# Attention and channel mix on one core: loads of steps 1 to 6 on ScalarE's queue, normalising ahead of the reciprocals, two sums of weight quadrants moved

## The chip, the cores and the metric

The kernel runs on one core of a Trainium2 chip. The metric is the device time of one launch in microseconds; three runs of the kernel before took 910.71, 912.52 and 915.9 us, the median is 912.52 us.

## The reference

What is computed, cut to what matters (8 batches, 12 heads, 448 tokens, head size 64, model 768, hidden 1024, all float32):

```
scores = q @ k.T / 8
scores = cap * tanh(scores / cap)
attn   = softmax(scores)                       # per head
x      = (attn @ v), heads side by side        # (8, 448, 768)
xprev  = x shifted by one token
xk = mu_k * x + (1 - mu_k) * xprev
xr = mu_r * x + (1 - mu_r) * xprev
k  = relu(xk @ w_k)
out = sigmoid(xr @ w_r) * ((k * k) @ w_v)
```

## The kernel before

The 96 heads are taken as 48 pairs. `run` calls `step(i)` for i from 0 to 54; step i works on several pairs at once: the scores, tanh and exponentials of pair i, the product with the values of pair i-1, the reciprocals of its row sums, and the normalising and token mix of pair i-2. From the end of step 6 on each step also issues four pieces K of six matmuls each of the key product `xk @ w_k` for a batch whose six pairs are done. Behind the steps comes a second part, 112 slots long, that makes `(k*k) @ w_v` and `xr @ w_r` by seven products of quadrants in the place of eight.

Each engine works its instructions off in the order in which they are issued. That order is written out by hand as lists of words: `EVEN_0` and `ODD_0` for steps 0 to 5, `STEP_7` for step 6 (the name counts from one), `EVEN_6`/`ODD_6` and `EVEN`/`ODD` after them, `LAST` for steps 48 and 49. A digit behind a word is the group g of the 448 keys: groups 0 to 2 hold 128 keys each, group 3 holds the last 64 keys of two pairs and stands in even steps.

The words that matter here, with engine and line:

- `S` (TensorE, L249, L242): scores of a group into one of two PSUM tiles `s`. `tanh` (ScalarE, L255) frees that tile; `exp` (ScalarE, L267) follows in place.
- `V` (TensorE, L278, L288): product with the values, into one of two PSUM tiles `pv`. The tile of pair i-3 is taken over by pair i-1 in step i.
- `red` (VectorE, L297): sums of the exponentials of a group. `f` (VectorE, L488 to L497): one fifth of the unpacking of a 64-bit weight piece; four of the five issue work for the pieces 1 to 5, five for the wide ones from piece 6 on.
- `gather` (four transfers on SyncE's queue, L303): brings the sums of pair i-1 into one tile; `recip` (VectorE, L307 to L314): their reciprocals; `rec_store` (SyncE's queue, L317): writes them to HBM; `rec_load` (two transfers on SyncE's queue, L326): reads them back, spread over the partitions, into the one tile `r`.
- `norm` (VectorE, L330): multiplies pair i-2's `pv` by `r`; `mix_old` (ScalarE, L340): the old token's share, written back into `pv`; `mix_new` (VectorE, L345): the sum, after which `pv` is free; `x_high` (L97) and `x_low` (L107), both on GpSimd: the split of the mixed value into two parts for the matmuls.
- `load_v`, `load_qk`, `weight_load` (SyncE's queue, L182, L178, L452): the bulky loads, 256 KB, 448 KB and 384 or 768 KB. `weight_abs` (ScalarE, L464) reads the weight piece first, `weight_sum` (GpSimd, L504) ends its unpacking.
- `qk_high` (GpSimd, L97; as `qk_rise` on ScalarE, L101) and `qk_low` (GpSimd, L107): the same split for q and k of pair i+2.
- Around steps 48 and 49: `quad_sum` (VectorE, L731), the sums of quadrants of w_v, issued by the words `f` there, four for each half k of the rows; `w2_splits` (L737 on ScalarE, L738 on VectorE), a generator with 14 pairs of a cast and a subtraction, called from `run` and from the word `prep`; `relu` (ScalarE, L426), which frees a PSUM tile `kps` of the key product.

SyncE's queue waits in order too: a transfer that is not ready holds back all that are issued behind it. A transfer issued on ScalarE's queue stands in line among ScalarE's own instructions.

Of the kernel before, what the change touches and what calls it, by code (L numbers as in the profile page):

```python
# [17 lines left out]
B, H, S, D = 8, 12, 448, 64  # L18
NP = H // 2
# [5 lines left out]
NPAIR = B * NP  # L25
# [4 lines left out]
P = 128  # L30
U32 = mybir.dt.uint32
# [5 lines left out]
HC = DM // 2  # L37
# [26 lines left out]
ODD_0 = """load_v gather rec_load x_store weight_load S0 S1 V0 S2 V1 V2 V3 red3 f f f f f tanh0 exp0 red0  # L64
weight_sum tanh1 exp1 weight_abs red1 recip rec_store qk_high qk_low tanh2 exp2 norm red2 mix_old mix_new x_high x_low
load_qk weight_store"""
EVEN_0 = ODD_0.replace("V1", "V1 S3").replace(" red3", "").replace("red2", "red2 tanh3 exp3").replace("mix_new", "red3 mix_new")
# [4 lines left out]
STEP_7 = """load_v gather rec_load x_store weight_load weight_low S0 S1 V0 S2 V1 S3 V2 V3 f f f f f tanh0 exp0 red0  # L72
weight_sum tanh1 exp1 red1 recip rec_store tanh2 qk_rise exp2 norm red2 K K K K qk_low weight_abs tanh3 exp3 mix_old red3 mix_new x_high x_low
load_qk rec_load"""
LAST = """gather V recip rec_store norm rec_load K mix_old relu k_store prep mix_new x_high x_low gate_old
K f f f f f gate_new relu k_store prep K prep K relu k_store prep x_store tail_open"""
# [6 lines left out]
class Body:  # L83
# [93 lines left out]
    def load_part(self, i, c):  # L177
        self.nc.sync.dma_start(self.raw[i][:, c], self.qk[i // NP, i % NP][:, c])  # L178

    def load_v(self, i):  # L180
        t = self.rawv[i] = self.rawp.tile([P, 4, 2, D], F32, name="rv", bufs=3)
        self.nc.sync.dma_start(t.rearrange("p c h d -> p (c h d)"), self.v[i // NP, i % NP])  # L182
# [564 lines left out]
    def step(self, i, KS):  # L747

        nk = nq = 0
        if self.maxima and i < NPAIR and i % 2 == 0:  # L750
            for j in (i, i + 1):
                self.row_maxima(j)
        pair = dict(load_qk=i + 4, qk_high=i + 2, qk_low=i + 2, qk_rise=i + 2, load_v=i, S=i, tanh=i, exp=i, red=i)
        pair.update(dict.fromkeys("V gather recip rec_store".split(), i - 1))
        pair.update(dict.fromkeys("norm mix_old mix_new x_high x_low gate_old".split(), i - 2))
        pair.update(x_store=i - 3, gate_new=i - 3)
        for op in ((EVEN_0, ODD_0) if i < 6 else (STEP_7,) if i == 6 else (EVEN_6, ODD_6) if i < REST[0] else (LAST, LAST) if NPAIR <= i < NPAIR + 2 else (EVEN, ODD))[i % 2].split():
            j = pair.get(op)
            op, g = (op[:-1], (int(op[-1]),)) if op[-1].isdigit() else (op, ())
            if op in pair:  # L760
                j = pair[op] if j is None else j
                if op == "load_qk" and i == 0:
                    self.load_qk(3)
# [9 lines left out]
            elif op == "tail_open":  # L773
                self.tail_open(i)
            elif op == "f":
                if i in (QUADS + 3, QUADS + 5):
                    self.quad_sum(i - QUADS - 3)
                elif i <= NPAIR:
                    self.fill()
            elif op == "quad_load":  # L780
                if QUADS <= i < QUADS + 4:
                    self.quad_load(2 * (i - QUADS) + nq)
                    nq += 1
            elif op == "relu_early":
                if i % NP == 2:
                    self.relu()
            elif op == "weight_load":
                if i + 1 in KEYS or i + 1 in REST:
                    self.weight_load()
            elif op == "weight_abs":  # L790
                if i == 0:
                    self.guard()
                elif i in KEYS or i in REST:
                    self.weight_abs()
            elif op == "weight_store":
                if i == 0:
                    self.weight_abs()
                self.weight_store()
            else:
                getattr(self, op)()  # L800

    def run(self):
        tc, nc = self.tc, self.nc
        KS = NF * ND * 3 // NP // 4
# [5 lines left out]
        with ExitStack() as outer:  # L810
# [57 lines left out]
            for i in range(NPAIR + LAG):  # L868
                if i == tail:
# [110 lines left out]
```

## Time and profile before

| | before |
|---|---|
| three runs, us | 910.71, 912.52, 915.9 |
| profiled execution, us | 912.79 |
| its span, us | 910.9 |
| TensorE busy | 882.2 us, 97% |
| VectorE busy | 728.7 us, 80% |
| ScalarE busy | 627.1 us, 69% |
| GpSimd busy | 410.3 us, 45% |
| mean granted TensorE clock | 0.988 |

The span runs from the first to the last instruction; the execution's own time is 1.9 us longer. Shares over the whole span hide the stages: in the first 70 us TensorE has the gaps, and VectorE, ScalarE and GpSimd are all three busy for most of the time; from about 70 us on TensorE has few gaps. In the rows, "PE" is TensorE, "DVE" VectorE, "ACT" ScalarE, "POOL" GpSimd, "SPq" and "ACTq" the queues on which SyncE and ScalarE issue transfers.

### The profile page before, as it was taken

Reading aid. Unit: us, or ns where it says so; the run is one execution under the profiler, and the core shown is the slowest. Engines: PE = TensorE matmul, PEld = TensorE weight load, DVE = VectorE, ACT = ScalarE, POOL = GpSimd, SP = SyncE. Lnnn points to the kernel's source line nnn. Section 1 sums busy time; section 2 is a strip of 40 time slices with the busy share of each in tenths; the row PEclk is TensorE's granted clock in tenths of the full one; section 3 lists DMA queues with packets and bytes.
Section 4 is the critical chain, followed back from the end, with each engine's and each line's share of the span. In section 5 each row is a group of like instructions: output and inputs, shape, how many; then the busy total and the mean of one; then the engine's idle time right before and its main releaser. Section 6 shows DMA issues by size and latency. Waiting matters only on the chain.

```text
span 910.9 us, 15206 instructions
## 1 busy us (share of the span) xinstructions
PE 882.2 (97%) x5034; PEld 695.8 (76%) x5034; DVE 728.7 (80%) x1246; ACT 627.1 (69%) x899; POOL 410.3 (45%) x345
## 2 busy tenths in 40 slices
PE   7879999999999999999999999999999999999996
PEld 3236666666666666666666789999999999999996
DVE  6889986988998898898868656788878767777875
ACT  8898887877888878877877366566565535555553
POOL 4996674776776676676763200000000014443330
PEclk8899999999999999999999999999999999999999
DMA  5566646666667766766555355745454546766663
GB/s 179 175 198 186 196 158 190 195 213 195 198 197 207 216 181 196 216 199 189 184 186 182 125 202 157 237 158 176 146 163 153 181 139 192 217 218 216 222 217 112
DMA packets 123672, 170.04 MB, mean 187 GB/s; under 512 B 22592, under 2 KB 107712, under 8 KB 123584
## 3 DMA queue, kind: packets, MB, share of 16 engines
q1 hardware_dynamic: 114224, 154.10, 55.4%
q10 hardware_dynamic: 9360, 14.88, 4.5%
q8 instruction: 42, 0.69, 0.3%
q14 instruction: 46, 0.38, 0.1%
HBM read 109.91 MB, written 56.60 MB: 183 GB/s over the span
## 4 chain that ended last, share of the span: by engine, by line
PE 77%; DVE 8%; DMA 6%; ACT 5%; issue 2%; SPq 2%; POOL 1%; DVEq 0%; ACTq 0%; POOLq 0%
PE ps L622 39%; PE kps L419 19%; PE pv L278 9%; PE s L249 8%; DMA sq__194<-r 2%; DVE r L297 2%; ACT p L255 2%; PE pv L288 2%; DMA rec_d<-rs 1%; PE s L242 1%; DMA r<-rec_d 1%; ACT p L267 1%; SPq L303 1%; DVE xk L345 1%; DVE sq__194 L307 1%
## 5 line engine op out<-in xcount | busy, mean ns | idle before, releaser
L297 DVE TRANSPOSE_TENSOR_REDUCE r<-p 128x28 f32<-128x896 f32 (+1 forms) x192 | 183.1, 975 | 19.6 <-ACT p L267 19.3
L255 ACT ACTIVATE p<-s,scl_t 128x896 f32<-128x896 f32 x168 | 165.4, 997 | 39.4 <-PE s L249 29.8
L267 ACT ACTIVATE p<-p,cap_t 128x896 f32<-128x896 f32 x168 | 173.7, 1040 | 7.8 <-ACT ko L426 2.5
L419 PE MATMUL kps<-xkh,wkh 128*128 128x448 f32 x372 | 142.5, 383 | 4.0 <-ACT ko L426 3.7
L419 PE MATMUL kps<-xkh,wkl 128*128 128x448 f32 x372 | 136.7, 368 | 0.6 <-POOL wkl L107 0.6
L419 PE MATMUL kps<-xkl,wkh 128*128 128x448 f32 x372 | 136.6, 367 | 0.0
L586 POOL TENSOR_TENSOR s<-src 128x384 f32<-128x384 f32 x14 | 14.2, 1017 | 270.6 <-DVE lo L607 262.2
L278 PE MATMUL pv<-p,rv 128*64 128x448 f32 x576 | 125.3, 566 | 8.8 <-DVE xk L345 8.8
L622 PE MATMUL ps<-wvh,hi 128*128 128x384 f32 x392 | 131.2, 335 | 0.2 <-ACT xl L384 0.2
L622 PE MATMUL ps<-wvl,hi 128*128 128x384 f32 x392 | 131.1, 335 | 0.0
L606 ACT CAST hi<-s 128x512 fp32r<-128x512 f32 (+1 forms) x112 | 63.6, 567 | 89.9 <-PE ps L622 76.6
L607 DVE TENSOR_TENSOR lo<-s,hi 128x512 fp32r<-128x512 f32 (+1 forms) x112 | 71.1, 635 | 59.2 <-ACT hi L606 43.4
L107 POOL TENSOR_TENSOR qkl<-rqk,qkh 128x896 fp32r<-128x896 f32 x47 | 100.4, 2136 | 8.5 <-ACT qkh L101 5.0
L622 PE MATMUL ps<-wrh,hi 128*128 128x384 f32 x294 | 98.7, 336 | 0.3 <-DVE o L645 0.3
L622 PE MATMUL ps<-wrl,hi 128*128 128x384 f32 x294 | 98.6, 335 | 0.0
L419 PEld LDWEIGHTS kps<-xkh,wkh 128*128 128x128 f32 x372 | 70.2, 189 | 26.7 <-issue 13.8
L278 PEld LDWEIGHTS pv<-p,rv 128*64 128x64 f32 x576 | 37.0, 139 | 70.1 <-issue 53.3
L606 ACT CAST hi<-src 128x512 fp32r<-128x512 f32 (+1 forms) x84 | 47.7, 568 | 62.0 <-PE ps L622 59.1
L504 POOL TENSOR_TENSOR wsq<-wa,wsq 128x384 f32<-128x384 f32 (+1 forms) x40 | 54.2, 1354 | 75.9 <-DVE wsq L497 53.9
L622 PE MATMUL ps<-wvh,lo 128*128 128x384 f32 x392 | 83.8, 334 | 0.0
L419 PEld LDWEIGHTS kps<-xkl,wkh 128*128 128x128 f32 x372 | 70.2, 189 | 6.6 <-DVE xkl L107 0.4
L249 PEld LDWEIGHTS s<-qkh 64*128 64x128 f32 x288 | 27.8, 188 | 61.9 <-issue 23.6
(111 smaller groups left out, 1805.7 us busy)
## 6 DMA issues: line engine op xcount, KB each, us to landing
rqk<-qk SPq DMA_DIRECT2D x47, 448.0 KB
k_d<-ko ACTq DMA_DIRECT2D x64, 224.0 KB
src<-k_d SPq DMA_DIRECT2D x56, 256.0 KB
rv<-v SPq DMA_DIRECT2D x48, 256.0 KB
r<-rec_d SPq DMA_DIRECT2D x96, 112.0 KB
v_d<-o SPq DMA_DIRECT2D x56, 192.0 KB
src<-x_d SPq DMA_DIRECT2D x42, 256.0 KB
vl<-v_d SPq DMA_DIRECT2D x56, 192.0 KB
```

Of the source, the lines that this page charges most:

```text
L107: {"p": self.nc.gpsimd, "v": self.nc.vector}[e].tensor_sub(*a)
L249: nc.tensor.matmul(s[:, (h + i) % 2, 0:S], qk[a][p, k], qk[b][p, 0:S], start=(n == 0), stop=(n == 2))
L255: self.nc.scalar.activation(p32, self.S.pop((i, g))[:, :, 0:S], AF.Tanh, scale=self.scl_t)
L267: self.nc.scalar.activation(p32, p32, AF.Exp, scale=1.0 if self.maxima else self.cap_t)
L278: nc.tensor.matmul(pv[p, 0:S], v[:, g, h, :], ph[:, (h + i) % 2, :], start=(g == 0), stop=False)
L288: nc.tensor.matmul(self.PV[j][p, 0:S], v[t, 3, h, :], ph[t, j % 2, :], start=False, stop=True)
L297: self.nc.vector.tensor_reduce(out=r1[:, 0:RM].rearrange("p (x g) -> p x g", g=3)[:, :, g] if g < 3 else r1[:, RM:RC], in_=p32.rearrange(" ...
L419: nc.tensor.matmul(self.kps[fc][:, 0:S], w, m[:, dc, :], start=first, stop=last)
L504: {"p": self.nc.gpsimd, "v": self.nc.vector}[e].tensor_add(sq, f(a), sq)
L606: self.nc.scalar.copy(hi, x)
L607: self.nc.vector.tensor_sub(lo, x, f(hi))
L622: self.nc.tensor.matmul(o, a[:, c, :], w[:, c, :], start=first and k == 0, stop=last and k == len(todo) - 1, skip_group_check=True)
```

## The change

In steps 0 to 6 the lists are written anew. In steps 1 to 6 the three bulky loads go out on ScalarE's queue (`self.bulk`): the values and the q and k of a pair behind the first exponential, the weight piece behind the second. The q and k are loaded for pair i+3 in the place of i+4, and step 7 loads two pairs. `norm`, `mix_old` and `mix_new` stand ahead of `recip`, and `rec_load` right behind `rec_store`, so that `norm` uses what the step before has loaded. In steps 3 and 5 `x_high` becomes `x_rise`, on ScalarE. At the end of the attention, two of the four quadrant sums of the second half go from step 48 to step 49, behind `norm`, and the three weight splits ahead of step 49 go behind it, so that seven stand there in the place of four.

```diff
-ODD_0 = """load_v gather rec_load x_store weight_load S0 S1 V0 S2 V1 V2 V3 red3 f f f f f tanh0 exp0 red0
-weight_sum tanh1 exp1 weight_abs red1 recip rec_store qk_high qk_low tanh2 exp2 norm red2 mix_old mix_new x_high x_low
-load_qk weight_store"""
-EVEN_0 = ODD_0.replace("V1", "V1 S3").replace(" red3", "").replace("red2", "red2 tanh3 exp3").replace("mix_new", "red3 mix_new")
+ODD_0 = """gather x_store S0 S1 V0 S2 V1 V2 V3 red3 f f f f f tanh0 exp0 load_v load_qk red0
+weight_sum tanh1 exp1 weight_load norm weight_abs red1 mix_old mix_new recip rec_store rec_load qk_high qk_low x_rise x_low tanh2 exp2 red2
+weight_store"""
+EVEN_0 = ODD_0.replace("V1", "V1 S3").replace(" red3", "").replace("x_rise", "x_high").replace("red2", "red2 tanh3 exp3 red3")
...
-STEP_7 = """load_v gather rec_load x_store weight_load weight_low S0 S1 V0 S2 V1 S3 V2 V3 f f f f f tanh0 exp0 red0
-weight_sum tanh1 exp1 red1 recip rec_store tanh2 qk_rise exp2 norm red2 K K K K qk_low weight_abs tanh3 exp3 mix_old red3 mix_new x_high x_low
-load_qk rec_load"""
+STEP_7 = """gather x_store weight_low S0 S1 V0 S2 V1 S3 V2 V3 f f f f f tanh0 exp0 load_v load_qk red0
+weight_sum tanh1 exp1 weight_load norm red1 mix_old mix_new recip rec_store rec_load x_high x_low tanh2 qk_rise exp2 red2 K K K K qk_low weight_abs tanh3 exp3 red3"""
 LAST = """gather V recip rec_store norm rec_load K mix_old relu k_store prep mix_new x_high x_low gate_old
-K f f f f f gate_new relu k_store prep K prep K relu k_store prep x_store tail_open"""
+K f f gate_new relu k_store prep K prep K relu k_store prep x_store tail_open""", \
+    """norm K mix_old f f mix_new x_high x_low relu k_store prep K relu k_store prep K prep K relu k_store prep x_store"""
...
-        self.nc.sync.dma_start(self.raw[i][:, c], self.qk[i // NP, i % NP][:, c])
+        self.bulk.dma_start(self.raw[i][:, c], self.qk[i // NP, i % NP][:, c])
...
+    def x_rise(self, i):
+        self.x_high(i, "s")
...
+        self.bulk = self.nc.scalar if 0 < i < 7 else self.nc.sync
...
-        pair = dict(load_qk=i + 4, qk_high=i + 2, qk_low=i + 2, qk_rise=i + 2, load_v=i, S=i, tanh=i, exp=i, red=i)
+        pair = dict(load_qk=i + (3 if i < 7 else 4), qk_high=i + 2, qk_low=i + 2, qk_rise=i + 2, load_v=i, S=i, tanh=i, exp=i, red=i)
...
-                if op == "load_qk" and i == 0:
-                    self.load_qk(3)
+                if op == "load_qk" and i == 7:
+                    self.load_qk(10)
...
-                if i in (QUADS + 3, QUADS + 5):
-                    self.quad_sum(i - QUADS - 3)
+                if i in (QUADS + 3, QUADS + 5, QUADS + 6):
+                    self.quad_sum(i - QUADS - 3 & 2)
...
-                    self.w2 = self.w2_splits()
-                    for _ in range(3):
-                        next(self.w2)
                 self.prep_now = i in (tail + 1, tail + 2)
                 self.step(i, KS)
...
                 if i == tail:
-                    for _ in range(4):
+                    self.w2 = self.w2_splits()
+                    for _ in range(7):
                         next(self.w2)
```

`load_v` and `weight_load` take `self.bulk` in the same way; `tail` is step 49 and QUADS is 43. Three places show how the instructions now stand.

ScalarE in step 3, before (`p_490`, `p_497` and `p_514` are the groups 0, 1 and 2 of pair 3, L464 is `weight_abs`, L340 is `mix_old` of pair 1):

```order
L255 ACTIVATE p_490<-s,scl_t 128x896
L267 ACTIVATE p_490<-p_490,cap_t 128x896
L255 ACTIVATE p_497<-s,scl_t 128x896
L267 ACTIVATE p_497<-p_497,cap_t 128x896
L464 ACTIVATE wsq<-w_356 128x384
L255 ACTIVATE p_514<-s,scl_t 128x896
L267 ACTIVATE p_514<-p_514,cap_t 128x896
L340 ACTIVATE pv<-x_163,om_k 128x448
```

ScalarE in step 3, with the change (the groups are `p_484`, `p_495` and `p_523`; lines are three higher from L351 on):

```order
L255 ACTIVATE p_484<-s,scl_t 128x896
L267 ACTIVATE p_484<-p_484,cap_t 128x896
L182 DMA rv<-v 128x512
L178 DMA rqk<-qk 128x896
L255 ACTIVATE p_495<-s,scl_t 128x896
L267 ACTIVATE p_495<-p_495,cap_t 128x896
L455 DMA w_498<-wk 128x3x256
L467 ACTIVATE wsq<-w_407 128x384
L340 ACTIVATE pv<-x_163,om_k 128x448
L101 CAST xkh<-xk 128x448
L255 ACTIVATE p_523<-s,scl_t 128x896
L267 ACTIVATE p_523<-p_523,cap_t 128x896
```

Three loads have come in, and `mix_old` and the cast `x_rise` stand ahead of the last tanh, where `mix_old` stood behind the last exponential.

VectorE in step 3, before, from the sums of group 0 (L297) to `mix_new` (L345):

```order
L297 TENSOR_REDUCE r_1_198<-p_490 128x28
L297 TENSOR_REDUCE r_1_198<-p_497 128x28
L307 TENSOR_REDUCE sq__194<-sq__194 32x2x14
L309 TENSOR_REDUCE sr_196<-sq__194 32x28
L312 RECIPROCAL sr_196<-sr_196 32x28
L314 STREAM_TRANSPOSE rs<-sr_196 32x32
L330 TENSOR_TENSOR x_163<-pv,r 128x448
L297 TENSOR_REDUCE r_1_198<-p_514 128x28
L345 SCALAR_TENSOR_TENSOR xk<-x_163,mu_k,pv 128x448
```

VectorE in step 3, with the change, the same nine instructions:

```order
L297 TENSOR_REDUCE r_1_198<-p_484 128x28
L330 TENSOR_TENSOR x_163<-pv,r 128x448
L297 TENSOR_REDUCE r_1_198<-p_495 128x28
L345 SCALAR_TENSOR_TENSOR xk<-x_163,mu_k,pv 128x448
L307 TENSOR_REDUCE sq__194<-sq__194 32x2x14
L309 TENSOR_REDUCE sr_196<-sq__194 32x28
L312 RECIPROCAL sr_196<-sr_196 32x28
L314 STREAM_TRANSPOSE rs<-sr_196 32x32
L297 TENSOR_REDUCE r_1_198<-p_523 128x28
```

`norm` (L330) and `mix_new` (L345) have gone ahead of the four instructions of `recip`; the instructions ahead of these rows, two half sums and the four of `f`, stand where they stood.

VectorE from `norm` of pair 46 to `x_low` of pair 47, steps 48 and 49, before (L731 are the quadrant sums, L738 the subtractions of the splits, L357 `gate_new`):

```order
L330 TENSOR_TENSOR x_161<-pv,r 128x448
L345 SCALAR_TENSOR_TENSOR xk<-x_161,mu_k,pv 128x448
L731 TENSOR_TENSOR w_5088<-w_5089,w_5088 128x768
L731 TENSOR_TENSOR wa<-w_5090,w_5088 128x768
L731 TENSOR_TENSOR w_5089<-w_5090,w_5089 128x768
L731 TENSOR_TENSOR wsq<-wsq,wa 128x768
L357 SCALAR_TENSOR_TENSOR xg<-x_163,mu_r,xg 128x448
L738 TENSOR_TENSOR wvl_5694<-wa,wvh_5705 128x768 x2
L738 TENSOR_TENSOR wvl_5693<-w_5088,wvh_5704 128x768
L330 TENSOR_TENSOR x_163<-pv,r 128x448
L345 SCALAR_TENSOR_TENSOR xk<-x_163,mu_k,pv 128x448
L107 TENSOR_TENSOR xkl<-xk,xkh 128x448
```

The same stretch with the change:

```order
L330 TENSOR_TENSOR x_161<-pv,r 128x448
L345 SCALAR_TENSOR_TENSOR xk<-x_161,mu_k,pv 128x448
L734 TENSOR_TENSOR w_5088<-w_5089,w_5088 128x768
L734 TENSOR_TENSOR wa<-w_5090,w_5088 128x768
L360 SCALAR_TENSOR_TENSOR xg<-x_163,mu_r,xg 128x448
L330 TENSOR_TENSOR x_163<-pv,r 128x448
L734 TENSOR_TENSOR w_5089<-w_5090,w_5089 128x768
L734 TENSOR_TENSOR wsq<-wsq,wa 128x768
L345 SCALAR_TENSOR_TENSOR xk<-x_163,mu_k,pv 128x448
L107 TENSOR_TENSOR xkl<-xk,xkh 128x448
```

Two sums and three subtractions no longer stand ahead of `norm` of pair 47; two sums stand between it and its `mix_new`, and the subtractions follow `x_low`.

On SyncE's queue a step from 3 to 6 now reads: the four transfers of `gather`, `x_store`, `rec_store`, the two of `rec_load`.

## Rows read from the trace of the kernel before

**Rows 1.** Stretches: length, busy us of PE, PEld, DVE, ACT, POOL, granted clock, DMA.
```profile
21.40:68.10 46.70, 38.15 (x204) 14.47 (x202) 40.62 (x70) 41.62 (x48) 43.23 (x39) 0.89 0.57 180
...
50.60:56.30 5.70, 5.70 (x34) 2.41 (x34) 5.53 (x10) 5.46 (x7) 5.45 (x6) 1.00 0.36 124
...
530.00:533.80 3.80, 3.71 (x11) 3.32 (x12) 3.32 (x5) 3.12 (x7) 0.00 (x0) 0.55 1.01 337
```

**Rows 2.** Waits in 20 to 70 us: who for whom, total us, times, longest.
```profile
PE pv L278 <- DVE xk L345: 7.8, 4, 3.0
...
DVE sq__194 L307 <- DMA sq__194<-r: 3.8, 2, 2.1
```

**Rows 3.** Timeline of ACT, steps 2 to 7: start, length, instruction [idle before].
```profile
21.38 1.01 ACT L255 ACTIVATE p<-s,scl_t 128x896 f32<-128x896 f32 x1 [0.60 <-PE s L249]
...
40.79 1.01 ACT L255 ACTIVATE p<-s,scl_t 128x896 f32<-128x896 f32 x1 [0.78 <-PE s L249]
...
44.75 0.55 ACT L464 ACTIVATE wsq<-w 128x384 f32<-128x384 f32 x1
...
57.29 0.64 ACT L340 ACTIVATE pv<-x,om_k 128x448 f32<-128x448 f32 x1 [1.14 <-DVE x L330]
...
68.08 1.01 ACT L255 ACTIVATE p<-s,scl_t 128x896 f32<-128x896 f32 x1 [0.20 <-PE s L249]
```

**Rows 4.** Timeline of DVE, steps 1, 5 and 8.
```profile
21.00 0.20 DVE L314 STREAM_TRANSPOSE rs<-sr 32x32 f32<-32x32 f32 x1
...
51.03 0.53 DVE L491 TENSOR_SCALAR kps<-wsq 128x384 uint32<-128x384 uint32 x1
...
53.25 2.10 DVE L297 TRANSPOSE_TENSOR_REDUCE r<-p 128x28 f32<-128x896 f32 x2
55.27 0.48 DVE L307 TENSOR_REDUCE sq__194<-sq__194 32x28 f32<-32x336 f32 x1
...
56.66 0.60 DVE L330 TENSOR_TENSOR x<-pv,r 128x448 f32<-128x448 f32 x1
...
58.20 0.64 DVE L345 SCALAR_TENSOR_TENSOR xk<-x,mu_k,pv 128x448 f32<-128x448 f32 x1
...
89.44 0.68 DVE L345 SCALAR_TENSOR_TENSOR xk<-x,mu_k,pv 128x448 f32<-128x448 f32 x1 [1.67 <-ACT pv L340]
```

**Rows 5.** Timeline of ACT's queue: two transfers issued beside an exponential.
```profile
87.77 0.88 ACTq L432 DMA_DIRECT2D k_d<-ko  x2
```

**Rows 6.** Chain that ended last: landings of reciprocals on the way out and back.
```profile
25.78 4.04 DMA r<-rec_d
...
102.55 2.83 DMA rec_d<-rs
...
105.96 3.05 DMA r<-rec_d
...
113.33 1.28 DMA rec_d<-rs
```

**Rows 7.** Timeline of SyncE's queue: the two loads of pair 47's reciprocals.
```profile
512.50 1.12 SPq L326 DMA_DIRECT2D r<-rec_d  x2
```

**Rows 8.** Timeline of PE: products with values of steps 5 and 7, and step 51.
```profile
50.60 0.97 PE L278 MATMUL pv<-p,rv 128*64 128x448 f32 x4 [1.52 <-DVE xk L345]
...
69.32 2.48 PE L278 MATMUL pv<-p,rv 128*64 128x448 f32 x12 [0.66 <-DVE xk L345]
...
530.09 0.50 PE L419 MATMUL kps<-xkh,wkh 128*128 128x448 f32 x1 [2.14 <-ACT ko L426]
```

**Rows 9.** Timeline of DVE, step 48.
```profile
513.05 0.95 DVE L731 TENSOR_TENSOR w<-w,w 128x768 f32<-128x768 f32 x1
...
517.86 0.67 DVE L357 SCALAR_TENSOR_TENSOR xg<-x,mu_r,xg 128x448 f32<-128x448 f32 x1
```

**Rows 10.** Timeline of ACT, the splits behind step 49.
```profile
523.63 2.30 ACT L737 CAST wvh<-w 128x768 fp32r<-128x768 f32 x3
...
529.51 0.96 ACT L426 ACTIVATE ko<-kps 128x448 f32<-128x448 f32 x2
```

More of the change, by code (lines that the diff above doesn't have):

```diff
@@ L177, in load_part @@
     def load_part(self, i, c):
-        self.nc.sync.dma_start(self.raw[i][:, c], self.qk[i // NP, i % NP][:, c])
+        self.bulk.dma_start(self.raw[i][:, c], self.qk[i // NP, i % NP][:, c])
     def load_v(self, i):
         t = self.rawv[i] = self.rawp.tile([P, 4, 2, D], F32, name="rv", bufs=3)
-        self.nc.sync.dma_start(t.rearrange("p c h d -> p (c h d)"), self.v[i // NP, i % NP])
+        self.bulk.dma_start(t.rearrange("p c h d -> p (c h d)"), self.v[i // NP, i % NP])
     def qk_high(self, i, e="p"):
@@ L451, in weight_load @@
             src = self.wk.bitcast(U32)[d[0] * P:(d[-1] + 1) * P, 2 * c * P:2 * (c + 1) * P]
-            self.nc.sync.dma_start(w.rearrange("p (c n) t -> p c (n t)", n=P), src.rearrange("(c p) n -> p c n", p=P))
+            self.bulk.dma_start(w.rearrange("p (c n) t -> p c (n t)", n=P), src.rearrange("(c p) n -> p c n", p=P))
         else:
@@ L456, in weight_load @@
             src, c = (self.wr, c) if c < ND else (self.wv, c - ND)
-            self.nc.sync.dma_start(w.rearrange("p n t -> p (n t)"), src.bitcast(U32)[c * P:(c + 1) * P, 2 * h * HC:2 * (h + 1) * HC])
+            self.bulk.dma_start(w.rearrange("p n t -> p (n t)"), src.bitcast(U32)[c * P:(c + 1) * P, 2 * h * HC:2 * (h + 1) * HC])
         self.w_raw.append((n, w))
@@ L752, in step @@
                 self.row_maxima(j)
-        pair = dict(load_qk=i + 4, qk_high=i + 2, qk_low=i + 2, qk_rise=i + 2, load_v=i, S=i, tanh=i, exp=i, red=i)
+        pair = dict(load_qk=i + (3 if i < 7 else 4), qk_high=i + 2, qk_low=i + 2, qk_rise=i + 2, load_v=i, S=i, tanh=i, exp=i, red=i)
         pair.update(dict.fromkeys("V gather recip rec_store".split(), i - 1))
-        pair.update(dict.fromkeys("norm mix_old mix_new x_high x_low gate_old".split(), i - 2))
+        pair.update(dict.fromkeys("norm mix_old mix_new x_high x_rise x_low gate_old".split(), i - 2))
         pair.update(x_store=i - 3, gate_new=i - 3)
-        for op in ((EVEN_0, ODD_0) if i < 6 else (STEP_7,) if i == 6 else (EVEN_6, ODD_6) if i < REST[0] else (LAST, LAST) if NPAIR <= i < NPAIR + 2 else (EVEN, ODD))[i % 2].split():
+        for op in ((EVEN_0, ODD_0) if i < 6 else (STEP_7,) if i == 6 else (EVEN_6, ODD_6) if i < REST[0] else LAST if NPAIR <= i < NPAIR + 2 else (EVEN, ODD))[i % 2].split():
             j = pair.get(op)
@@ L803, in run @@
         tc, nc = self.tc, self.nc
+        self.bulk = nc.sync
         KS = NF * ND * 3 // NP // 4
```

## The prediction

> **What bounds the kernel now.** I read first the stretches, to find where TensorE is not full, then the waits there, then each engine's timeline step by step. In the stretch of steps 2 to 6, from 21.4 to 68.1 us, TensorE is busy for 38.2 of 46.7 us, while VectorE (40.6), ScalarE (41.6) and GpSimd (43.2) are each near full [rows 1]: three engines of nearly the same load, coupled step by step. TensorE's own wait there is for `mix_new`, which frees the tile of the products: 7.8 us in 4 waits [rows 2]. VectorE waits 3.8 us for gathered sums [rows 2]. From step 7 on TensorE is nearly full, so what these steps take longer or shorter is handed on to the end, as far as TensorE feels it.
>
> ScalarE's step starts are the reader's ruler: step 2 starts at 21.38, step 4 at 40.79, step 6 behind the instruction at 57.29, step 7 at 68.08 [rows 3]. A tanh and an exponential together take 1.98 us (two pairs from 40.79 to 44.75). ScalarE waits where `mix_old` waits for `norm`, 1.14 us in step 5 [rows 3].
>
> **The change, steps 1 to 6.** The durations on VectorE [rows 4]: the four of `f` 2.22 us (51.03 to 53.25), a sum `red` 1.01 (two until 55.27), `recip` 1.39 (until 56.66), `norm` 0.60, `mix_new` 0.64; a half-size sum I put at 0.55, an estimate from the 1.01. `mix_old` is 0.64 [rows 3].
>
> Before, `mix_old` was ScalarE's last work of a step, so nothing but its own queue stood between the groups. Now it stands ahead of the third tanh, and so do, on VectorE, the last sum of the step before, the four of `f`, the sum of group 0 and `norm`. That chain starts when the last exponential of the step before ends.
> - Even step: 1.01 + 2.22 + 1.01 + 0.60 = 4.84 us until `norm` is done. ScalarE would be there after two pairs and `weight_abs`, about 4.4, so it waits 0.4. Then `mix_old` 0.64 and two pairs 3.96: 9.44 us.
> - Odd step: two half sums, 2.22, 1.01, 0.60 make 4.93. Then the sum of group 1 and `mix_new`, 6.58; `x_rise` waits for that and takes about as long as `mix_old` on the same size, 7.2; one pair more: 9.2 us.
> - Step 2 waits for pair 0's reciprocals. They leave VectorE at 21.2 [rows 4], as before, since step 1 does nothing else there. The way out and back: landing 1.28 to 2.83 us from the issue of `rec_store`, 0.5 for the first `rec_load`, half of 1.12 [rows 7], and 3.05 to 4.04 from there [rows 6]: 4.9 to 7.4 us. I take 5.3, near the lower end, since no bulky load stands ahead on this queue any more. That is 5.1 into the step; with `norm`, `mix_old` and two pairs, 10.3 us.
> - Step 6: its ScalarE work is unchanged and had hardly a gap, 10.2 us (57.9 to 68.08). It now waits from 3.96, where two pairs are done, to 4.84: 11.1.
>
> Sum: 10.3 + 9.2 + 9.44 + 9.2 + 11.1 = 49.2 where 46.7 stood: step 7 starts 2.5 us **later** on ScalarE, at 70.6. Steps 3 to 5 pay for an early `norm` with waits on ScalarE.
>
> TensorE feels less of it. Its first products of step 7 started at 69.32, the last 0.66 of that a wait for `mix_new` [rows 8], and that wait goes. Now the second score group ahead of them waits for the tile that the last tanh of step 6 frees, 1 us ahead of step 7: 69.6. Six matmuls at 2.48 / 12 us each [rows 8] are 1.2 at most: 70.8, so **+1.5 us**. VectorE starts step 7 some 2 us late, but waits 1.67 us in step 8 for `mix_old` [rows 4], which takes up the rest. Bounds of this term: -0.7 (only the wait goes) to +2.5 (all of ScalarE's delay).
>
> What I cost at nothing:
> - The 18 loads in ScalarE's line. Two transfers took 0.88 us to issue [rows 5], beside an exponential; behind one they are covered. Uncovered, 3 x 0.44 a step less the 0.4 that ScalarE waits anyway would be 0.9 us a step, some 4.5 in all: the upper end. None has a buffer to wait for: each takes over a tile whose last reader was issued a step or more before.
> - `rec_load` holding SyncE's queue. It waits there for the landing of `rec_store`, and `gather` stands behind it. Counted from the end of a `recip`: 1.7 landing, 1.12 for `rec_load`, 2.2 for four issues at half of 1.12, and a landing of 2.2 between the 1.28 and 3.05 of [rows 6]: 7.2. The next `recip` starts 9.2 - 1.39 = 7.8 later. Cover 0.6; above that it is late.
> - `x_high` leaving GpSimd in steps 3 and 5: its splits of q and k were ready ahead of need.
>
> **The change, steps 48 and 49.** TensorE stood 2.14 us at 530.09 for a tile that `relu` frees [rows 8], and `relu` at 529.51 stood behind eight splits, 0.735 us each from 523.63 [rows 10]. After it the clock fell: 530 to 533.8 ran at 0.55 [rows 1]. Four sums took 4.81 us from 513.05 to 517.86 [rows 9]. With two there and `gate_new`, VectorE is free at 516.1; the loads of pair 47's reciprocals go out at 512.5 [rows 7], 0.5 + 3.05 later they are in: also 516.1. `norm` 516.7, `mix_old` beside two sums 519.1, `mix_new` 519.75, `x_high` 520.4. Then seven splits and four more from `prep`, eleven in all, 8.1 us: `relu` starts at 528.5 in place of 529.5. **-1.05 us**, and the gap shrinks to 1.1 us, or somewhat more where TensorE arrives sooner. A gap of 1.52 us [rows 8] was followed by a clock of 1.00, 50.6 to 56.3 [rows 1]; the one of 2.14 by 0.55. Mine is nearer to the first, so the clock holds: 0.45 x 3.8 = **-1.7 us**. Bounds: 0 (reciprocals 1 us later) to -2.75. The subtractions on VectorE end about when they did, so nothing behind is later.
>
> **Sum** against the profiled execution: 912.79 + 1.5 - 2.75 = **911.5 us**, 1.0 below the median of 912.52. The profiled execution lies 0.27 above that median. I take half a per cent, 4.6 us, as what a measurement of this kernel can tell from no change: below 908.0 faster, above 917.1 slower. Forecast: the same. With the bounds of both terms, 909.3 to 915.3.
>
> **Rivals.** *Slower: the reciprocals come late.* After a `recip` ends, 8.0 us into an odd step, the next `norm` wants them at 9.2 + 4.3: 5.5 us later; after an even step 5.9. At 5.3 they just fit. At the upper end, 7.4, each step waits 1.5 or 1.9, step 2 waits 2.1: 8.9 over five steps, 920.4 us; it passes half a per cent from about 6.6 us on. For it: both ends are measured in this kernel, and the bulky loads are still under way at the same time. Against it: 4.04 and 2.83 were taken with such loads ahead on the same queue. The Trainium skill, DMA: Bandwidth & Descriptors, section "Issuing engines are not separate DMA queues", has transfers from either queue run on the same 16 DMA engines and interleave, which would leave the landings where they were. No row of the kernel before shows the two queues loaded together; by that rule this rival holds. The same page's section on queues, rings and completion order lets each DMA engine take turns between queues, packet by packet, by which the small ones would pass: the forecast's 5.3.
>
> *Faster: ScalarE paces.* If the chain on VectorE is shorter than I sum it and no wait is left on ScalarE, its busy 41.6 us [rows 1] and two `x_rise` make 42.9: step 7 starts at 64.3, products some 0.2 later, 64.5 in place of 69.3, and 912.79 - 4.8 - 2.75 = 905.2 us. It takes about 60% of that to pass half a per cent. For it: ScalarE, TensorE and VectorE all had waits here, and the change aims at each. Against it: the order shows the four of `f` and two sums still ahead of `norm`, and their 4.8 us exceed ScalarE's 4.4.
>
> *Nothing happens in steps 1 to 6* because GpSimd, busy 43.2 of 46.7 [rows 1], holds the splits of q and k: then -2.75 alone, 910.0, still the same.
>
> **How the numbers follow.** Forecast 0.60, the third rival 0.08, slower 0.16, faster 0.16. The faster rival's lower part and the slower one's upper part are the 2 in 10 left out: 907 to 918. Faster by over 0.5%: 0.16; within: 0.68; slower: 0.16.
>
> **What would show it.** Right, step by step: ScalarE's `mix_old` waits for `norm` in every step from 2 to 6, and the third tanh follows it; step 7 starts near 70.6; TensorE's waits for `mix_new` in 20 to 70 us are gone; two transfers beside an exponential leave no gap; the gap ahead of the fifth key tile of the last batch is under 1.6 us and the clock in the 4 us behind it is 1.00. Wrong: a `norm` that waits for the landing of `r` in more than step 2 (the slower rival), step 7 before 67 us (the faster one), or a gap of 2 us with a lower clock behind it.

## The result, and the profile after

| | before | after |
|---|---|---|
| median, us | 911.73 (4 runs, 910.71 to 915.9) | 921.79 (4 runs, 920.66 to 924.04) |
| ratio | | 1.0105, 95% interval 1.0066 to 1.0144 |
| profiled execution, us | 912.79 | 920.8 |
| its span, us | 910.9 | 919.0 |
| mean granted clock | 0.988 | 0.985 |

The kernel before has one run more here than ahead of the prediction. The change makes the kernel slower by about 1%, 10 us; 911.5 was forecast, with 918 as the upper end. The profiled executions are 8.1 us of span apart.

Where these 8.1 us lie is read on TensorE, whose first twelve products with values in a step can be set side by side. The timeline of TensorE before, steps 7 (that one is in [rows 8]) and 8:

```profile
79.00 2.48 PE L278 MATMUL pv<-p,rv 128*64 128x448 f32 x12
```

The same products after, steps 7 and 8, and the one later stop, step 51:

```profile
74.70 4.13 PE L278 MATMUL pv<-p,rv 128*64 128x448 f32 x12
86.03 2.48 PE L278 MATMUL pv<-p,rv 128*64 128x448 f32 x12
...
538.25 0.47 PE L422 MATMUL kps<-xkh,wkh 128*128 128x448 f32 x1 [3.83 <-ACT ko L429]
```

At step 7 TensorE is 5.4 us late (74.70 to 69.32). The twelve products then take 4.13 us in place of 2.48, and from step 8 on it is 7.0 us late. It stays so to the last such products, of step 47 (512.32 to 505.21). The last 1.0 has come by the reciprocals of pair 47, which start at 517.77 in place of 509.68, ahead of all the work that the new tail moves. The stretches of steps 2 to 6, of these slow products and behind the late stop (columns as in [rows 1]):

```profile
20.90:74.80 53.90, 40.70 (x206) 15.26 (x204) 42.51 (x73) 43.02 (x50) 44.54 (x39) 0.87 0.51 163
74.80:79.00 4.20, 4.20 (x14) 1.21 (x16) 3.92 (x7) 3.99 (x5) 0.00 (x0) 0.59 0.40 120
538.20:542.00 3.80, 3.75 (x13) 3.40 (x14) 3.80 (x6) 3.34 (x6) 0.00 (x0) 0.68 0.56 194
```

Steps 2 to 6 take 53.9 us where 46.7 stood [rows 1] and 49.2 were forecast. The work in them is nearly the same; it is waits that grew, on every engine. The products of step 7 run at a granted clock of 0.59, which is mostly the lower of its two levels (1.2 of 2.4 GHz).

VectorE's timeline shows the wait, at the ends of the odd steps' reciprocals (L314) and the `norm` (L330) of the step behind:

```profile
21.58 0.20 DVE L314 STREAM_TRANSPOSE rs<-sr 32x32 f32<-32x32 f32 x1
28.25 0.62 DVE L330 TENSOR_TENSOR x<-pv,r 128x448 f32<-128x448 f32 x1 [2.23 <-DMA r<-rec_d]
...
41.24 0.20 DVE L314 STREAM_TRANSPOSE rs<-sr 32x32 f32<-32x32 f32 x1
...
47.46 0.63 DVE L330 TENSOR_TENSOR x<-pv,r 128x448 f32<-128x448 f32 x1 [0.42 <-DMA r<-rec_d]
...
60.79 0.20 DVE L314 STREAM_TRANSPOSE rs<-sr 32x32 f32<-32x32 f32 x1
68.15 0.63 DVE L330 TENSOR_TENSOR x<-pv,r 128x448 f32<-128x448 f32 x1 [1.80 <-DMA sq__194<-r]
```

From the end of a reciprocal to `norm` it is 6.5 (21.78 to 28.25), 6.0 and 7.2 us. 5.3 had been assumed. (The last wait is put down to a gather, but `norm` reads no sums: it waits for the counters of the two halves of `r`, whose loads went out from 64.09 on, and the second lands at 68.03.) The chain that ended last has the two legs of the first and the second of these; SyncE's queue shows the third's store and the loads that wait for it:

```profile
21.81 1.30 DMA rec_d<-rs
23.12 4.74 DMA r<-rec_d
...
41.47 1.25 DMA rec_d<-rs
43.33 3.93 DMA r<-rec_d
```

```profile
61.01 0.31 SPq L317 DMA_DIRECT2D rec_d<-rs  x1
64.09 1.12 SPq L326 DMA_DIRECT2D r<-rec_d  x2
```

The way out is short, as hoped, for the first two; for the third it is 3.1 us (61.01 to 64.09). On the way back a load of half of `r` takes 4.7 and 3.9 us, no less than with the bulky loads ahead on the same queue (4.04 and 3.05 in [rows 6]). From the first of the two loads to `norm` it is 5.1, 4.7 and 4.1 us, where 0.5 + 3.05 stood in the sum. Behind the late `norm` comes ScalarE, with a second stop of its own. Its timeline in step 2 and its step starts:

```profile
20.89 0.99 ACT L255 ACTIVATE p<-s,scl_t 128x896 f32<-128x896 f32 x1
...
27.94 0.39 ACTq L455 DMA_DIRECT2D w<-wk  x1
28.37 0.55 ACT L467 ACTIVATE wsq<-w 128x384 f32<-128x384 f32 x1 [3.42 <-DMA r<-rec_d]
...
33.43 0.99 ACT L255 ACTIVATE p<-s,scl_t 128x896 f32<-128x896 f32 x1
...
42.55 0.99 ACT L255 ACTIVATE p<-s,scl_t 128x896 f32<-128x896 f32 x1
...
52.74 0.99 ACT L255 ACTIVATE p<-s,scl_t 128x896 f32<-128x896 f32 x1
...
61.86 0.99 ACT L255 ACTIVATE p<-s,scl_t 128x896 f32<-128x896 f32 x1
...
74.81 0.99 ACT L255 ACTIVATE p<-s,scl_t 128x896 f32<-128x896 f32 x1
```

The steps take 12.54, 9.12, 10.19, 9.12 and 12.95 us. The odd ones are the forecast's 9.2; the even ones are 2.2, 0.75 and 1.85 longer than its 10.3, 9.44 and 11.1. And `weight_abs` (L467), which needs nothing of `r`, stands 3.42 us for its landing: the load of weights (L455) ahead of it in ScalarE's line went out only at 27.94. In the built program a transfer has one of eight completion counters (a semaphore that tells of its landing) in turn, whichever queue it is on, and is held until the transfer eight issues earlier has landed. For this load that is the first half of `r`, which lands at 27.86. The stop itself costs hardly anything here: `mix_old`, next in ScalarE's line, waits for `norm`, which ends at 28.87.

### The profile page after: what moved, and what is told of

It is laid out like the page before. It is cut to its first block, busy times and chain, and to the rows that moved or that the text cites. A ratio compares the mean times of both kernels' runs of the same rounds, so it can differ in the third digit from the quotient of the medians.

```text
span 919.0 us, 15199 instructions
## 1 busy us (share of the span) xinstructions
PE 885.4 (96%) x5034; PEld 696.4 (76%) x5034; DVE 726.3 (79%) x1246; ACT 627.7 (68%) x901; POOL 408.5 (44%) x343
## 4 chain that ended last, share of the span: by engine, by line
PE 80%; ACT 6%; DMA 6%; DVE 5%; issue 1%; SPq 1%; POOL 0%; ACTq 0%; DVEq 0%; POOLq 0%
PE ps L625 38%; PE kps L422 21%; PE pv L278 9%; PE s L249 8%; ACT p L255 2%; DMA sq__194<-r 2%; PE pv L288 2%; PE s L242 1%; DVE r L297 1%; DMA r<-rec_d 1%; ACT p L267 1%; DMA rec_d<-rs 1%; ACT wvh L740 1%; ACT ko L429 1%; DMA wvl<-w_d 1%
## 5 line engine op out<-in xcount | busy, mean ns | idle before, releaser
L297 DVE TRANSPOSE_TENSOR_REDUCE r<-p 128x28 f32<-128x896 f32 (+1 forms) x192 | 183.5, 975 | 21.4 <-ACT p L267 20.8
L610 DVE TENSOR_TENSOR lo<-s,hi 128x512 fp32r<-128x512 f32 (+1 forms) x112 | 70.6, 630 | 59.6 <-ACT hi L609 44.3
L609 ACT CAST hi<-src 128x512 fp32r<-128x512 f32 (+1 forms) x84 | 47.6, 567 | 61.2 <-PE ps L625 58.2
L249 PE MATMUL s<-qkh 64*128 64x448 f32 x288 | 65.7, 452 | 18.6 <-ACT p L255 10.4
```

The costliest lines, as they stand in the source:

```text
L249: nc.tensor.matmul(s[:, (h + i) % 2, 0:S], qk[a][p, k], qk[b][p, 0:S], start=(n == 0), stop=(n == 2))
L297: self.nc.vector.tensor_reduce(out=r1[:, 0:RM].rearrange("p (x g) -> p x g", g=3)[:, :, g] if g < 3 else r1[:, RM:RC], in_=p32.rearrange(" ...
L609: self.nc.scalar.copy(hi, x)
L610: self.nc.vector.tensor_sub(lo, x, f(hi))
```

## The experiments

Twelve kernels, in three sets, each beside the kernel before (medians 912.21, 912.01 and 912.21). "Step 7" and "step 8" say how many us after 69.32 and 79.00 the first products with values of these steps start in the profiled execution; where the second is larger by 0.9 or more, the products of step 7 ran at a low clock. The profiled execution is one of the runs, for `r` from v the fastest (916.45), for the old tail the slowest (922.51).

| run | median, us | ratio, 95% | step 7 | step 8 |
|---|---|---|---|---|
| the change | 921.79 | 1.0066 to 1.0144 | 5.4 | 7.0 |
| loads on SyncE | 921.66 | 1.0062 to 1.0135 | 7.1 | 8.8 |
| old tail | 919.21 | 1.0039 to 1.0086 | 6.9 | 8.6 |
| new tail alone | 912.71 | 0.9986 to 1.0022 | -0.9 | -0.9 |
| mixing at the end | 923.69 | 1.0069 to 1.0151 | 10.6 | 12.3 |
| `r` from v | 920.35 | 1.0077 to 1.0122 | 3.2 | 4.8 |
| reciprocals first | 934.54 | 1.0235 to 1.0282 | 21.4 | 22.3 |
| `norm` first alone | 917.56 | 1.0051 to 1.0088 | 5.4 | 5.4 |
| ScalarE's queue alone | 915.17 | 1.0023 to 1.0053 | 2.2 | 2.3 |
| `r` of pair 0 | 919.71 | 1.0060 to 1.0107 | 6.0 | 6.0 |
| the same, weights on SyncE | 919.12 | 1.0050 to 1.0085 | 4.8 | 6.3 |
| weights on SyncE | 919.35 | 1.0054 to 1.0094 | 4.8 | 4.8 |
| `r` of pair 0, all on SyncE | 916.12 | 1.0028 to 1.0059 | 1.4 | 1.4 |

Theory 1 was at first: the way of the reciprocals, out and back, ends last. Theory 2: the loads in ScalarE's line.

**Loads back on SyncE's queue.**

```
-        self.bulk = self.nc.scalar if 0 < i < 7 else self.nc.sync
+        self.bulk = self.nc.sync
```

> The change with the bulky loads of steps 1 to 6 back on SyncE's queue, at the places where the new lists issue them; order of norm, mix and reciprocals as changed. Theory 1 (the reciprocals come too late for an early norm, and the third tanh stands behind norm): nothing of the loss goes, 918 to 922 us, steps 2 to 6 on ScalarE still take 52 to 55 us where the kernel before takes 46.7. Theory 2 (the loads in ScalarE's line hold ScalarE: its weight load waits for the landing of the reciprocals and all behind it stands): the three waits of 3.4, 1.0 and 2.9 us ahead of weight_abs go, 912 to 915 us.

921.66 us, as with the change: to move the loads back gives nothing, against theory 2. The chain that ended last, the store that step 6 waits for:

```profile
60.81 5.55 DMA rec_d<-rs
```

and VectorE's `norm` behind it:

```profile
69.85 0.63 DVE L330 TENSOR_TENSOR x<-pv,r 128x448 f32<-128x448 f32 x1 [3.44 <-DMA sq__194<-r]
```

Now the small store takes 5.55 us, behind three bulky loads issued on its queue from 58.2 to 59.6 us; the way back is 3.5 (66.38 to 69.85). In all 9.1 us from the end of the reciprocals, 7.2 with the change. In steps 2 and 4 it is 6.2 and 6.3 us, 6.5 and 6.0 with the change: there time moves from one leg to the other.

| us, `norm` of step | 2 | 4 | 6 |
|---|---|---|---|
| the change: from the store to the loads of `r`, from there to `norm` | 1.3, 5.1 | 1.3, 4.7 | 3.1, 4.1 |
| loads on SyncE: the same | 1.9, 4.2 | 2.8, 3.5 | 5.6, 3.5 |

**The tail as before; the new tail alone.** In the first, `LAST`, the branch of `quad_sum` and the calls of `w2_splits` are before's in the changed kernel; in the second the reverse.

```
-                if i in (QUADS + 3, QUADS + 5, QUADS + 6):
-                    self.quad_sum(i - QUADS - 3 & 2)
+                if i in (QUADS + 3, QUADS + 5):
+                    self.quad_sum(i - QUADS - 3)
...
```

> The change in steps 0 to 6, but quadrant sums, splits and list of steps 48 and 49 as before. By the trace of the change its products with values run 7.1 us behind the kernel before up to step 48 and its key product of the last batch 8.15 us behind afterwards, so the new end costs about 1 us: 920 to 921 us, gap ahead of the fifth key tile back near 2.1 us. By the forecast's term the new end gains 1.0 to 2.7 us: 922.5 to 924.5 us. If the 1 us is chance of one execution: no difference, 921 to 922 us.

> The kernel before with only the end of steps 48 and 49 changed. By the forecast's term 909 to 911 us; by the reading of the change's trace (the reciprocals of pair 47 land some 5 us after their load is issued, norm of pair 47 waits for them, relu stands behind eleven splits) about 1 us slower than before, 912 to 913.5 us, with a gap of 3 to 4 us ahead of the fifth key tile.

With the old tail 919.21 us, below all three figures named, its interval overlapping the change's; the new tail alone is no different from before, 1.0004. So the loss is in steps 0 to 6, and the tail's forecast gain isn't there. Why, by the second's timelines of VectorE, ScalarE and TensorE:

```profile
517.23 0.63 DVE L331 TENSOR_TENSOR x<-pv,r 128x448 f32<-128x448 f32 x1 [1.37 <-DMA r<-rec_d]
...
528.76 0.96 ACT L427 ACTIVATE ko<-kps 128x448 f32<-128x448 f32 x2
...
529.35 0.47 PE L420 MATMUL kps<-xkh,wkh 128*128 128x448 f32 x1 [2.91 <-ACT ko L427]
```

This execution is 0.86 us ahead at the reciprocals of pair 47 (508.82 against 509.68). The loads of `r` go out at 511.64, and `norm` waits for them to 517.23: 5.6 us, 0.5 + 3.05 assumed. `relu` at 528.76 is then 0.75 ahead of 529.51, 0.1 later than the lead alone gives. TensorE, which ends its work ahead of the stop 1.5 us sooner than before, stands 2.91 us, and the clock is low behind it as before.

**Mixing back at the end of the step**, loads on ScalarE's queue, `norm` first:

```
-weight_sum tanh1 exp1 weight_load norm weight_abs red1 mix_old mix_new recip rec_store rec_load qk_high qk_low x_rise x_low tanh2 exp2 red2
+weight_sum tanh1 exp1 weight_load norm weight_abs red1 recip rec_store rec_load qk_high qk_low tanh2 exp2 red2 mix_old mix_new x_rise x_low
```

> The change with mix_old and mix_new of steps 1 to 6 back behind the last exponential (x_rise, x_high behind them), norm still ahead of recip, loads still on ScalarE's queue. Theory 1: ScalarE's third tanh no longer stands behind norm, steps 2 to 6 take 46 to 48.5 us, 912 to 915 us. Theory 2: the weight load is still in ScalarE's line ahead of the third tanh and still waits for the landing of the reciprocals, so ScalarE still stands some 3 us in steps 2 and 6: 917 to 921 us.

923.69 us: theory 1's forecast for it fell, and theory 2's 921 is passed. ScalarE's timeline, step 3:

```profile
38.11 0.33 ACTq L178 DMA_DIRECT2D rqk<-qk  x1
38.50 1.01 ACT L255 ACTIVATE p<-s,scl_t 128x896 f32<-128x896 f32 x1 [4.97 <-DMA r<-rec_d]
```

A tanh stands 4.97 us behind a load of q and k that itself waits for `r`. With the early mixing that stop is hidden, since `mix_old` waits for the same `r`; without it, it shows. So both theories have a part, and theories A (the way of `r`) and D (both, one behind the other) were put to the next two sets.

**`r` that waits for nothing.** In the first, `r` of pairs 0 to 5 is read from the input v; its output has other magnitudes, and its six times spread from 916.45 to 922.61, so its trace is used.

```
+    def r_early(self, i):
+        r = self.up.tile([P, S], F32, name="r", bufs=1)
+        for h in range(2):
+            self.nc.sync.dma_start(r[HALF[h]], self.v[i // NP, i % NP][h:h + 1, 0:S].to_broadcast([64, S]))
+        self.R[i] = r
...
-weight_sum tanh1 exp1 weight_load norm weight_abs red1 mix_old mix_new recip rec_store rec_load qk_high qk_low x_rise x_low tanh2 exp2 red2
+weight_sum tanh1 exp1 weight_load norm weight_abs red1 mix_old mix_new r_early recip rec_store rec_load qk_high qk_low x_rise x_low tanh2 exp2 red2
```

> The change, but in steps 1 to 6 the tile r of pairs 0 to 5 is loaded from rows of the input v, behind mix_new and ahead of recip, in place of the stored reciprocals (so these six pairs are normalised by other numbers; the reciprocals are still computed and stored). Same size and number of loads, but nothing to wait for. Theory A: the loop recip, rec_store, rec_load, norm, mix_new, recip paces steps 2 to 6, since norm now stands ahead of recip and its r is out and back in 6.0 to 7.2 us; a turn is 9.6 us. Then no norm waits for r in steps 2 to 6, the steps take the 49.2 us of the prediction or less, the first twelve products with values of step 7 start near 70 to 71 us (74.7 with the change), and the time is 912 to 916 us. Theory B: the early mixing chain on VectorE and ScalarE is what is long, and the waits for r only lie beside it: products at 73 us or later, 919 to 922 us.

No `norm` waits for `r` in steps 2 to 6, yet step 7 is still 3.2 us late: by this trace A's part is 2.2 of 5.4. ScalarE stood 0.55 to 1.75 us ahead of the weights in each step (a load of weights, and what it waited for). The second reads the stored reciprocals of pair 0 for pairs 1 to 5 (`self.rec_d[0]` in `r_early`), and pair 0 its own; two more move loads in it.

> The change, but in steps 2 to 6 the tile r of pairs 1 to 5 is loaded from the stored reciprocals of pair 0, behind mix_new and ahead of recip (these five pairs are normalised by pair 0's sums; their own reciprocals are still computed and stored). As the run with r from v, with numbers of the usual size. Theory D (two causes, one behind the other: norm's wait for r, and behind it ScalarE standing at the load of weights that it issues itself, 0.5 to 1.7 us a step ahead of weight_abs): the first products of step 8 start 4 to 5.5 us after the 79.0 us of before (86.0 with the change), 916 to 919 us. Theory A (r alone): within 1.5 us of 79.0, 911 to 914 us.

> As r of pair 0, and the loads of weights of steps 1 to 6 go out on SyncE's queue at the same place of the program (values, q and k stay on ScalarE's). Theory D: ScalarE's gaps ahead of weight_abs fall under 0.3 us each, products of step 8 within 2 us of 79.0, 911 to 914.5 us: below the run with r of pair 0 by 2 us or more. Theory A: no different from the run with r of pair 0.

> As r of pair 0, and all bulky loads of steps 1 to 6 on SyncE's queue at their places of the change. Theory D: as with the weights alone on SyncE's queue, 911 to 914.5 us, if the queue as such costs nothing. Theory E: on one queue the gathered sums and r stand behind the bulky loads, so recip waits for gather by 1 us or more in several steps: 915 to 920 us.

With `r` of pair 0 and the loads on ScalarE's queue: 919.71 us, 6.0 late at both steps: A's 911 to 914 us is out, D's ends, 919 us and 5.5 late, are passed by a little, since pair 0 waits 3.09 us for its own `r`. ScalarE in step 4, the load of weights held:

```profile
49.06 0.41 ACTq L463 DMA_DIRECT2D w<-wk  x1
49.57 0.54 ACT L475 ACTIVATE wsq<-w 128x384 f32<-128x384 f32 x1 [1.99 <-POOL wkl L107]
```

With the weights' loads on SyncE's queue these stops are gone, as D said, but not the time, against it: pair 0 waits for its own `r`, 4.40 us in step 2, and starts 7.3 us behind the first load of it (22.74 to 30.06), and the clock is low at step 7 (3.89 us for the twelve products). With all loads on SyncE's queue the same `norm` waits 1.2 us. That kernel's step starts and two of its `mix_old` on ScalarE, steps 2 to 7, and its products on TensorE, steps 7 and 8:

```profile
21.51 1.01 ACT L255 ACTIVATE p<-s,scl_t 128x896 f32<-128x896 f32 x1 [0.64 <-PE s L249]
...
32.00 0.99 ACT L255 ACTIVATE p<-s,scl_t 128x896 f32<-128x896 f32 x1
...
37.09 0.64 ACT L348 ACTIVATE pv<-x,om_k 128x448 f32<-128x448 f32 x1 [0.60 <-DVE x L338]
...
41.13 0.98 ACT L255 ACTIVATE p<-s,scl_t 128x896 f32<-128x896 f32 x1
...
50.68 0.99 ACT L255 ACTIVATE p<-s,scl_t 128x896 f32<-128x896 f32 x1
...
59.81 0.99 ACT L255 ACTIVATE p<-s,scl_t 128x896 f32<-128x896 f32 x1
...
64.85 0.64 ACT L348 ACTIVATE pv<-x,om_k 128x448 f32<-128x448 f32 x1 [1.00 <-DVE x L338]
...
70.86 0.98 ACT L255 ACTIVATE p<-s,scl_t 128x896 f32<-128x896 f32 x1
```

```profile
70.73 2.48 PE L278 MATMUL pv<-p,rv 128*64 128x448 f32 x12
80.40 2.48 PE L278 MATMUL pv<-p,rv 128*64 128x448 f32 x12
```

Here the prediction's chain stands as it was summed: steps of 10.49, 9.13, 9.55, 9.13 and 11.05 us (49.35; forecast 49.2) and products at 70.73 (70.8). Beside the run with all loads on SyncE's queue and each pair's own `r`, it is the plainest pair of the series: to open the loop of `r` takes off 5.5 us (921.66 to 916.12), and step 7 is 1.4 us late in place of 7.1. The median, 916.12, is above D's 914.5, and within E's 915 to 920, but not by E's waits: no `recip` of steps 2 to 6 waits for `gather`. 1.4 us are lost by step 8 and some 2.4 more in the tail of the profiled execution, where TensorE stands 3.88 us.

**Weights alone on SyncE's queue**, `r` as in the change (`self.nc.sync` in place of `self.bulk` in the two loads of `w`):

> The change with one edit: the loads of weights of steps 1 to 6 go out on SyncE's queue at the same place of the program. Theory D: norm still waits for its own r, and mix_old behind it, so that taking only the second cause away gives back under 2.5 us: 918.5 to 922 us. If ScalarE's own loads were the main cause: 912 to 916 us.

919.35 us, as D has it: with its stop taken away, `norm` still waits for `r` (2.67, 0.38 and 1.21 us).

**The order alone.** The reciprocals ahead of `norm` in the changed kernel:

```
-weight_sum tanh1 exp1 weight_load norm weight_abs red1 mix_old mix_new recip rec_store rec_load qk_high qk_low x_rise x_low tanh2 exp2 red2
+weight_sum tanh1 exp1 weight_load recip rec_store norm rec_load weight_abs red1 mix_old mix_new qk_high qk_low x_rise x_low tanh2 exp2 red2
```

> The change, but recip and rec_store stand ahead of norm again in steps 1 to 7 (rec_load right behind norm); loads on ScalarE's queue, early mixing and x_rise stay. Theory A: the loop is open, since a recip no longer waits for the norm before it: norm has over 8 us for its r, waits for r at most in step 2, products of step 7 start at 69 to 71.5 us, 911 to 916 us; recip may then wait 1 to 2 us for gather, as before. Theory B (the early mixing is what costs): 919 to 922 us as with the change.

934.54 us: worst of all, against A. VectorE's and ScalarE's timelines, step 4:

```profile
55.59 0.49 DVE L307 TENSOR_REDUCE sq__194<-sq__194 32x28 f32<-32x336 f32 x1 [2.77 <-DMA sq__194<-r]
...
56.97 0.60 DVE L330 TENSOR_TENSOR x<-pv,r 128x448 f32<-128x448 f32 x1
```

```profile
57.60 0.64 ACT L340 ACTIVATE pv<-x,om_k 128x448 f32<-128x448 f32 x1 [4.54 <-DVE x L330]
```

The loop of `r` is open, but another is closed: last exponential, last sum, gather, `recip`, `norm`, `mix_old`, and behind `mix_old` the third tanh. A turn is 13.3 us (`norm` at 43.66 and 56.97); the four from step 2 to step 6 take 12.2 to 14.5. So with the mixing early, `norm` has to be first. The next run has `norm` first without the early mixing.

In the kernel before, `norm` ahead of `recip` and `rec_load` right behind `rec_store`, nothing else:

> The kernel before with one edit: in steps 1 to 7 norm moves ahead of recip, and rec_load goes right behind rec_store; mixing late, loads on SyncE's queue and in their old places, old tail. Theory A: this edit alone closes the loop: norm waits for r in three or more of steps 2 to 6, products of step 7 start 3 us or more after the 69.3 of before, 916 to 922 us. Theory B: without the early mixing nothing is lost: 911 to 914.5 us.

917.56 us, 5.4 late, within A's figures, but not by A's wait: `norm` waits once, 0.18 us. VectorE's timeline, step 6, and SyncE's queue:

```profile
71.09 0.51 DVE L307 TENSOR_REDUCE sq__194<-sq__194 32x28 f32<-32x336 f32 x1 [2.82 <-DMA sq__194<-r]
```

```profile
61.81 0.34 SPq L317 DMA_DIRECT2D rec_d<-rs  x1
64.08 1.12 SPq L326 DMA_DIRECT2D r<-rec_d  x2
65.30 0.54 SPq L178 DMA_DIRECT2D rqk<-qk  x1
65.93 0.37 SPq L182 DMA_DIRECT2D rv<-v  x1
66.39 2.44 SPq L303 DMA_DIRECT2D sq__194<-r  x4
```

`rec_load` waits for the store, and `gather` stands behind it and behind the loads; `recip` waits for `gather` in five steps, 10.3 us.

**ScalarE's queue alone**: before's lists, `self.bulk` in the four loads.

> The kernel before with one edit: the bulky loads (values, q and k, weights) of steps 1 to 6 go out on ScalarE's queue, in their old places. Theory A: no loop, and the queue is not the cause: within 2.5 us of before, 910 to 914.5 us. Theory C: a load that ScalarE issues has to wait for the landing of a small transfer of SyncE's queue issued before it, and ScalarE stands there, 3 us in step 2 of the change: with it alone ScalarE shows gaps of 1 us and more ahead of loads in several steps, and the time is 915 to 920 us.

915.17 us, slower by 0.2 to 0.5%: A's upper end is passed; the time is within C's, but C's gaps aren't there (0.8 us is the longest at a load). It is a gather that lands late, by VectorE's timeline in step 5 and TensorE's in step 6:

```profile
56.74 0.49 DVE L307 TENSOR_REDUCE sq__194<-sq__194 32x28 f32<-32x336 f32 x1 [2.60 <-DMA sq__194<-r]
```

```profile
60.36 1.76 PE L278 MATMUL pv<-p,rv 128*64 128x448 f32 x4 [5.21 <-DVE xk L345]
```

Its four transfers were issued from 48.73 to 51.17, a moment behind three bulky loads of the other queue (47.04 to 48.35); the sums were there 5.6 us later.

## Why the prediction was wrong

- **"I take 5.3, near the lower end, since no bulky load stands ahead on this queue any more."** This step failed. 6.0 to 7.2 us were measured, inside the 4.9 to 7.4 named. The way back was sized at 0.5 + 3.05 and took 4.1 to 5.1; the store was short in the first two waits, 1.30 and 1.25 us, but held the loads for 3.1 in the third, beyond the 2.83 named. The sign given for this came: `norm` waits for `r` in steps 2, 4 and 6 (2.23, 0.42 and 1.80 us). The slower rival was built on this very leg and had a chance of 0.16; its mechanism deserved more, as only an argument about the queue stood against it.
- **The rival's 920.4 us** is close to the profiled 920.8, but in part by luck. It put 8.9 us on waits in five steps. Three steps waited and were 4.8 us longer than forecast, 3.9 on TensorE. The rest of the 9.3 us above 911.5 is the slow products of step 7, 1.65 us, and the end of the attention, 1.0 lost where the new tail was to gain 2.75.
- **The two rules on queues.** The landings of `r` did not get shorter, 4.74 and 3.93 us, and a gather landed late behind loads of the other queue with ScalarE's queue alone. This agrees with the Trainium skill, DMA: Bandwidth & Descriptors, section "Issuing engines are not separate DMA queues", by which transfers of either queue run on the same engines and interleave. The store of the reciprocals did get shorter, 1.3, 1.3 and 3.1 us where it was 1.9, 2.8 and 5.6 with the loads on its queue. This fits the turns between queues that the Trainium skill states on the same page, in the section on queues, rings and completion order. That the loads of `r` would pass by such turns too, as was forecast, no run shows.
- **The loads "costed at nothing. None has a buffer to wait for."** Issuing behind an exponential did cost nothing, as said. But a load has more to wait for than a buffer: the landing eight issues earlier. Step 7 was 1.4 us late with neither cause (`r` of pair 0, all on SyncE), 3.2 with the loads' alone (`r` from v), 4.8 with the way of `r` alone (weights on SyncE) and 5.4 with both, as in the change: less than their sum, since `mix_old` and the load wait for the same landing. These shares are rough: with `r` of pair 0 step 7 was 6.0 and 4.8 us late, as pair 0 itself then waited 3.09 and 4.40 us.
- **The chain on VectorE and ScalarE, +1.5 us,** was right to a tenth where nothing else held it (70.73 for 70.8; 49.35 for 49.2). Even there it is a loss, 49.35 us where 46.7 stood: no run shows a gain by the early mixing in these steps.
- **The clock.** No term held a change of it at step 7, where the twelve products took 4.13 us in place of 2.48: 1.65 us.
- **The tail, -2.75:** measured 1.0004 for it alone. Failed at the same place, the landing of `r`, 3.05 assumed and about 5 measured; the bound of 0 ("reciprocals 1 us later") was the right one, and as the stop stayed long, the clock behind it stayed low. The trace of the kernel before had this price: by its counter the second half of pair 47's `r` lands there at 517.97, 5.5 us behind the first load's issue at 512.50, which no wait shows, as `norm` starts at 521.06. The eleven splits took 8.07 us (529.59 to 537.66), as forecast.
- "`rec_load` holding SyncE's queue", with a cover of 0.6 us: with the change the waits for `gather` stayed under 0.25 us, with `norm` later still; with `norm` first alone that cover was gone, 10.3 us of waits.

What is open: whether some order of the small transfers and the bulky ones fits them all into a step of 9.4 us. None of those tried did, and none of the kernels beats the one before.

## What to carry to other kernels

Before an operation is moved ahead of its producer's, close the loop on paper: store, load and use of a small result that goes through HBM is a chain with a length of its own, and moving the use earlier can make the step as long as the chain. Price its legs at the slowest landing that the trace shows while the bulky loads run, whichever queue they are on, landings that nothing waits for included. And a transfer put into a computing engine's line brings its own waits there, those for older transfers too.

## What the runs showed of the hardware

- A second queue moves time between a small transfer's legs. With the bulky loads on ScalarE's queue the reciprocals took 1.3, 1.3 and 3.1 us out and 5.1, 4.7 and 4.1 back, with them on SyncE's 1.9, 2.8 and 5.6 out and 4.2, 3.5 and 3.5 back. The way as a whole was no shorter in steps 2 and 4 (6.5 and 6.0 against 6.2 and 6.3), and 1.9 us shorter in step 6 (7.2 against 9.1).
- ScalarE stood 3.42 and 4.97 us at loads of its own that were held for the landing of `r` on SyncE's queue, which the instruction behind them doesn't read.
- The length of the stop ahead doesn't tell alone what clock is granted. Ahead of step 7's products TensorE stood 2.49, 2.48 and 2.42 us for a tanh with the change, with `r` of pair 0 and with the weights on SyncE; the twelve products took 4.13, 2.48 and 2.48 us. The prediction's reading of the tail, 1.00 behind 1.52 us and 0.55 behind 2.14, was of the same kind. What decides is open.
